# A start without unread matmuls between the first scores, and the first weights behind the first pair

## The chip, the cores and the metric

The kernel runs on one core of a Trainium2 chip. The metric is the device time of one launch in microseconds (us): the median over several executions. The engines of the core are named as in the profile: PE (TensorE, with PEld for its weight loads), DVE (VectorE), ACT (ScalarE), POOL (GpSimd) and SP (SyncE, which issues the DMAs here). Each runs its own list of instructions in order.

## What is computed

Attention with a forget gate for 8 batches of 8 heads, 576 positions, 64 dimensions a head, and then a two-layer feed-forward network over the 4608 tokens:

```python
scores = scale * np.matmul(q, k.transpose(0, 1, 3, 2))
log_f = np.log(np.clip(f, 0.0001, 1.0))
cum = np.cumsum(log_f, axis=-1)
decay = cum[:, :, :, None] - cum[:, :, None, :]
scores = np.where(causal, -1000000000.0, scores + decay)
scores = scores - np.max(scores, axis=-1, keepdims=True)
attn = np.exp(scores)
attn = attn / (np.sum(attn, axis=-1, keepdims=True) + 1e-09)
x = np.matmul(attn, v)            # heads side by side: 4608 x 512
h = x @ w_in                      # 512 x 2048
g = np.maximum(0.01 * h, h)
return g @ w_out                  # 2048 x 512
```

All is float32. The two weight matrices arrive as 64-bit integers.

## The kernel before

**The opening.** Batches are taken in the order 0, 3, 4, 5, 6, 7, 1, 2. Of the first three, only the first 256 positions are done at first, so that the feed-forward network gets its first tokens soon. This is the loop at line 732: twelve *pairs* of heads, four for each of the three batches. For each pair `early_load` (L287) fetches q, k and v. `early_scores` (L298) makes four score tiles, two heads by two row blocks of 128. Each is a matmul of q and k, the "q·k part" (`sce<-qk`), and a second one that adds the decay (`sce<-both`, "decay part"). DVE then adds the mask, reduces to the row's extreme and writes tile `ze` (L323), and ACT takes the exponential and the row sum (L327). When a pair's four tiles are done, DVE scales them by the inverse sums (L336; from the fifth pair on ACT does it, L338). `early_values` (L340), one pair later, transposes them on PE (`tre`), copies them (`pte`), multiplies by v (`ave`) and splits the result in a high and a low part (`xh`, `xl`), which the network's matmuls read.

**The weights** come in 16 pieces, w_in and w_out in turn. A piece is loaded raw (`wraw`, two DMAs of 512 KB at L167) into one of two buffers, used in turn: piece n + 2 can be loaded only when piece n has been read for the last time. `load_weight` (L169) turns it into two float tiles, high and low (`win_h`, `win_l`, `wout_h`, `wout_l`). ACT does L181 and L192. DVE does L185, L194, L195 for the first five pieces, and L187, L206, L207, L210, L211 for the others. For the first five pieces PE also sums three products into PSUM (`ws`, L201 to L203), and ACT and DVE copy one half each back (L204). The tile `wt` in the middle has one buffer, so the pieces pass through one after the other. The first two pieces are fetched ahead of the loop. `WQ` says how many pieces come behind each pair's scores: one each for the first eight pairs, then two. Piece 0 is worked on ahead of the loop, by `weights(1)` in L731.

**The network** is cut into quanta (`ffn`, L617): groups of 256 tokens; for each of eight pieces p of the hidden layer, matmuls into `h`, the activation `g` on ACT (L654), its split `gh`, `gl` (L657, L659), and matmuls into `o`. `fill` (L700) puts quanta behind each pair, from the fifth on, by the table `FQ`. After the opening comes the loop over the remaining heads (L755), with quanta between all steps.

**Unread matmuls.** `warm(n)` (L119) multiplies a tile of zeros into a PSUM tile that nobody reads. `WARM = (20, 2, 6)` asks for 20 of them at the very start, and for 2 behind each of the two row blocks of each of the first 6 pairs (L330).

**The order.** A scheduling layer places the instructions of each engine, in the order of the program as far as its own plan of readiness allows. Since the unread matmuls depend on nothing but a free PSUM tile, 20 of the 24 later ones were placed around pair 0's first scores, the last four at pair 5's.

Of the kernel before, what the change touches and what calls it, by code (L numbers as in the profile page):

```python
# [28 lines left out]
FQ = (0, 0, 0, 0, 4, 8, 8, 8, 8, 8, 8, 4, 2)  # L29
BUFS = dict(s1=2, m1=2, ost=2)  # L30
RAWS = ("ph", "pl")
WARM = (20, 2, 6)
SCALED = 4
SUMMED = 5
NEG = -1.0e30
# [5 lines left out]
def forgetting_attention_ffn(ctx, tc, qT, kT, v4, vr, f, w_in, w_out, out):  # L41
# [77 lines left out]
    def warm(n):  # L119

        ps = psum.tile([P, 512], F32, tag="h", name=f"warm_{len(warmed)}")
        warmed.append(n)
        for _ in range(n):
            matmul(ps, still[:, :P], still, start=True, stop=True)

    warm(WARM[0])
    eye = one.tile([P, P], F32, tag="part0", name="eye")
# [36 lines left out]
    def fetch_weight(n):  # L164
        raw = raws[n] = one.tile([P, 2, 4 * P, 2], I32, tag=RAWS[n % 2], name=f"wraw_{n}")
        for k, src in enumerate(wpieces[n][0]):
            nc.sync.dma_start(raw[:, k].rearrange("p w two -> p (w two)"), src)  # L167
# [47 lines left out]
    def weights(n):  # L215
        while len(loaded) < min(n, len(wpieces)):
            load_weight(len(loaded))
# [80 lines left out]
    def early_scores(b, g):  # L298
# [3 lines left out]
        for i in range(2):  # L302
# [14 lines left out]
            for o in range(2):  # L317
# [11 lines left out]
                )  # L329
            if b * HPB // 2 + g < WARM[2]:  # L330
                warm(WARM[1])
        nc.vector.tensor_scalar(sm, sm, 1.0e-9, None, op0=ALU.add)
# [395 lines left out]
    early_load(0, 0)  # L728
    for n in range(len(RAWS)):
        fetch_weight(n)  # L730
    weights(1)  # L731
    for x, (b, g) in enumerate(steps + [(NE, 0)]):
        if x + 1 < len(steps):
            early_load(*steps[x + 1])
# [91 lines left out]
```

## Time and profile before

| | |
|---|---|
| median of 3 executions | 1208.28 us (1208.0 to 1208.91) |
| the profiled execution | 1209.36 us |
| its span, first to last instruction | 1207.5 us |
| PE busy | 1194.9 us, 7828 matmul records |
| DVE busy | 613.2 us |
| ACT busy | 633.2 us |
| unread matmuls, all 44 | 13.2 us of PE's records |

A row of the timeline reads: start, duration, engine, line, operation, output <- input, shapes, count, and in brackets the idle time of the engine ahead of it with what ended it. Matmuls overlap: the duration of a merged row reaches past the start of the next row, so a stretch of PE is measured from one row's start to the next one's. A float32 matmul that isn't marked fp32r shows as two records.

### The profile page before, as it was taken

How to read it: one execution, taken by the hardware profiler on the slowest of the kernel's cores; microseconds unless marked ns; L12 is line 12 of the kernel's file. 1: busy time of each engine (PE TensorE's matmuls, PEld its weight loads, DVE VectorE, ACT ScalarE, POOL GpSimd, SP SyncE). 2: the span in 40 equal slices, each digit the busy share in tenths (PEclk: the TensorE clock that was granted, in tenths of full speed). 3: DMA queues.
4: the chain of work that ended last, by engine and by line, in shares of the span. 5: the costliest groups of instructions: out<-in, count | busy, mean ns of one | idle time of the engine just before them, and what ended most of it. 6: DMA issues, size and time to landing. Idle time of an engine off the chain costs nothing.

```text
span 1207.5 us, 22521 instructions
## 1 busy us (share of the span) xinstructions
PE 1194.9 (99%) x7828; PEld 1068.1 (88%) x7828; DVE 613.2 (51%) x1697; ACT 633.2 (52%) x1622; POOL 460.8 (38%) x473
## 2 busy tenths in 40 slices
PE   9999999999999999999999999999999999999998
PEld 6678888888899999999999999999999999998997
DVE  6888365566655555464544445444443434553221
ACT  5887465666755565555554545455444445552111
POOL 2000255555455445454435354444354543531000
PEclk9999999999999999999999999999999999999999
DMA  6565233334343233323332223232233223311000
GB/s 202 175 204 177 78 99 101 99 111 118 102 137 82 82 99 101 99 72 97 87 96 79 80 66 101 65 100 59 69 85 93 58 71 81 80 58 52 13 18 19
DMA packets 82130, 110.57 MB, mean 92 GB/s; under 512 B 20640, under 2 KB 51728, under 8 KB 82016
## 3 DMA queue, kind: packets, MB, share of 16 engines
q1 hardware_dynamic: 82016, 109.12, 31.2%
q8 instruction: 63, 1.03, 0.4%
q14 instruction: 51, 0.42, 0.1%
HBM read 65.32 MB, written 18.58 MB: 69 GB/s over the span
## 4 chain that ended last, share of the span: by engine, by line
PE 95%; DVE 2%; ACT 1%; DMA 1%; issue 1%; POOL 0%; SPq 0%; DVEq 0%; ACTq 0%; POOLq 0%
PE h L111 34%; PE o L111 33%; PE tr L115 8%; PE av L111 8%; PE sc L111 7%; PE sce L111 2%; PE ave L111 1%; PE ws L111 1%; PE warm L111 1%; PE tre L115 1%; DVE fixed_z L437 1%; DMA wraw<-in_w_in 0%; ACT g L654 0%; DVE pl L489 0%; DVE gh L657 0%
## 5 line engine op out<-in xcount | busy, mean ns | idle before, releaser
L659 POOL TENSOR_TENSOR gl<-g,gh 128x512 fp32r<-128x512 f32 x113 | 148.8, 1317 | 275.1 <-DVE gh L657 270.1
L111 PE MATMUL o<-wout_h,gh 128*128 128x512 f32 x576 | 231.3, 402 | 0.0
L111 PE MATMUL o<-wout_l,gh 128*128 128x512 f32 x576 | 227.4, 395 | 0.0
L111 PE MATMUL o<-wout_h,gl 128*128 128x512 f32 x576 | 227.1, 395 | 0.0
L443 ACT ACTIVATE fixed_z<-fixed_z,max 128x192 f32<-128x192 f32 (+3 forms) x272 | 161.0, 592 | 101.4 <-DVE max L437 99.1
L111 PE MATMUL h<-xh,win_h 128*128 128x256 f32 x1152 | 206.2, 286 | 0.0
L487 ACT CAST ph<-tr 128x192 fp32r<-128x192 f32 (+3 forms) x360 | 126.7, 373 | 148.5 <-PE tr L115 99.2
L111 PE MATMUL h<-xh,win_l 128*128 128x256 f32 x1152 | 200.3, 283 | 0.0
L437 DVE CUSTOM_DVE_ANT_0 fixed_z<-sc,tri 128x192 f32<-128x192 f32 (+3 forms) x272 | 122.4, 451 | 151.3 <-PE sc L111 148.4
L654 ACT ACTIVATE g<-h 128x512 f32<-128x512 f32 x144 | 85.8, 596 | 216.1 <-PE h L111 211.0
L657 DVE CAST gh<-g 128x512 fp32r<-128x512 f32 x144 | 72.4, 503 | 217.6 <-ACT g L654 215.9
L489 DVE TENSOR_TENSOR pl<-tr,ph 128x384 fp32r<-128x384 f32 (+3 forms) x296 | 137.3, 467 | 80.7 <-ACT ph L487 79.5
L111 PEld LDWEIGHTS h<-xh,win_h 128*128 128x128 f32 x1152 | 170.8, 190 | 5.8 <-issue 0.5
L111 PEld LDWEIGHTS h<-xh,win_l 128*128 128x128 f32 x1152 | 164.8, 190 | 0.5 <-issue 0.2
L111 PE MATMUL h<-xs,win_h 128*128 128x256 f32 x1024 | 164.4, 283 | 0.0
L115 PE MATMUL tr<-ident_r,fixed_z 128*128 128x128 f32 x888 | 145.3, 273 | 3.4 <-DVE ph L494 1.7
L111 PEld LDWEIGHTS h<-xs,win_h 128*128 128x128 f32 x1024 | 141.0, 191 | 0.0
L115 PEld LDWEIGHTS tr<-ident_r,fixed_z 128*128 128x128 f32 x888 | 107.6, 140 | 25.2 <-ACT rb L566 5.2
L111 PEld LDWEIGHTS o<-wout_h,gl 128*128 128x128 f32 x576 | 108.2, 188 | 24.4 <-DVE maxe L323 0.3
L111 PEld LDWEIGHTS o<-wout_l,gh 128*128 128x128 f32 x576 | 108.7, 189 | 16.0 <-issue 0.5
L111 PEld LDWEIGHTS o<-wout_h,gh 128*128 128x128 f32 x576 | 108.9, 189 | 14.8
L154 POOL TENSOR_TENSOR fixed_m2a<-raw,m 64x576 fp32r<-64x576 f32 x32 | 46.6, 1458 | 195.4 <-ACT m L399 173.8
(130 smaller groups left out, 1753.2 us busy)
## 6 DMA issues: line engine op xcount, KB each, us to landing
raw<-in_kT SPq DMA_DIRECT2D x64, 144.0 KB
m<-m SPq DMA_DIRECT2D x64, 144.0 KB
wraw<-in_w_in SPq DMA_DIRECT2D x16, 512.0 KB
wraw<-in_w_out SPq DMA_DIRECT2D x16, 512.0 KB
fixed_vm<-in_v SPq DMA_DIRECT2D x64, 128.0 KB
xs<-xd SPq DMA_DIRECT2D x16, 512.0 KB
out<-ost SPq DMA_DIRECT2D x28, 256.0 KB
raw<-in_qT SPq DMA_DIRECT2D x40, 144.0 KB
```

What stands on the lines that cost most here:

```text
L111: nc.tensor.matmul(*args, **kw)
L115: nc.tensor.transpose(*args)
L154: nc.gpsimd.tensor_tensor(out, a, b, op=ALU.subtract)
L437: nc.vector.tensor_tensor_reduce(out=z[:, a:b], in0=ps[:m, :b - a], in1=tri[:m, at:at + b - a], scale=-SCALE, scalar=3.0e38 if x == 0 else ...
L443: nc.scalar.activation(z, z, AF.Exp, bias=h["max"][:m, last:last + 1], scale=-1.0, accum_out=fixed["sum" + "ab"[s // 2 % 2]][:m, i, s % 2: ...
L487: nc.scalar.copy(strided(ph, run), source(ps, run))
L489: nc.vector.tensor_tensor(strided(pl, run), source(ps, run), strided(ph, run).bitcast(F32), op=ALU.subtract)
L654: nc.scalar.activation(g, ph, AF.Prelu, alpha=0.01)
L657: nc.vector.tensor_copy(gh, g)
L659: eng.tensor_tensor(gl, g, gh.bitcast(F32), op=ALU.subtract)
```

## The change

Two edits. The table `WARM` becomes (20, 0, 0): the 20 unread matmuls at the very start stay, the 24 behind the row blocks of the first six pairs are gone. And `weights(1)` ahead of the loop is gone, so that piece 0 is worked on where the loop asks for it, behind pair 0's scores. The load of pieces 0 and 1 stays ahead of the loop.

```diff
@@ -29,7 +29,7 @@
 FQ = (0, 0, 0, 0, 4, 8, 8, 8, 8, 8, 8, 4, 2)
 BUFS = dict(s1=2, m1=2, ost=2)
 RAWS = ("ph", "pl")
-WARM = (20, 2, 6)
+WARM = (20, 0, 0)
 SCALED = 4
 SUMMED = 5
 NEG = -1.0e30
@@ -728,7 +728,6 @@
     early_load(0, 0)
     for n in range(len(RAWS)):
         fetch_weight(n)
-    weights(1)
     for x, (b, g) in enumerate(steps + [(NE, 0)]):
         if x + 1 < len(steps):
             early_load(*steps[x + 1])
```

The scheduling layer places all else anew. On PE, the list around pair 0's first scores was this, from the last of nine rows of two unread matmuls that stood behind the two q·k parts (`sce` with `_0` and `_2` are the first row block's scores, `_1` and `_3` the second's):

```order
L111 MATMUL warm_511<-still 128x512 x2
L111 MATMUL sce_0_0_216<-both 128x128
L111 MATMUL sce_0_2_217<-both 128x128
L111 MATMUL warm_526<-still 128x512 x2
L111 MATMUL sce_0_1_231<-qk_0_182 128x256
L111 MATMUL sce_0_3_232<-qk_0_182 128x256
L111 MATMUL ws_0_199<-wt_193,ident_r 128x512
```

and it is now:

```order
L111 MATMUL sce_0_0_200<-qk_0_182 128x128
L111 MATMUL sce_0_2_201<-qk_0_182 128x128
L111 MATMUL sce_0_0_200<-both 128x128
L111 MATMUL sce_0_2_201<-both 128x128
L111 MATMUL sce_0_1_212<-qk_0_182 128x256
L111 MATMUL sce_0_3_213<-qk_0_182 128x256
L111 MATMUL sce_0_1_212<-both 128x256
L111 MATMUL sce_0_3_213<-both 128x256
L111 MATMUL sce_1_0_253<-qk_1_193 128x128
```

The four scores of pair 0 now stand together, pair 1's follow at once, and piece 0's sums (`ws`) stand behind pair 1's four scores. Further changes of the order, on DVE, are shown in the prediction at the places where it speaks of them. From the first head of the second loop on, the lists of PE are the same again.

## The prediction

> **What bounds the kernel now.** I read the page first, for the engine that carries the span.
>
> ```profile
> span 1207.5 us, 22521 instructions
> PE 1194.9 (99%) x7828; PEld 1068.1 (88%) x7828; DVE 613.2 (51%) x1697; ACT 633.2 (52%) x1622; POOL 460.8 (38%) x473
> PE 95%; DVE 2%; ACT 1%; DMA 1%; issue 1%; POOL 0%; SPq 0%; DVEq 0%; ACTq 0%; POOLq 0%
> ```
>
> PE is busy 99% of the span, and 95% of the chain that ended last runs on it. So an edit at the start is worth what it takes off the time at which PE gets through the same list of matmuls, and nothing else. Then I read the stretches of the opening.
>
> ```profile
> 13.30:45.60 32.30, 31.36 (x140) 17.87 (x139) 26.97 (x87) 24.67 (x63) 0.00 (x0) 1.00 0.53 172
> 45.60:57.20 11.60, 11.60 (x85) 9.76 (x84) 10.82 (x25) 8.67 (x19) 0.00 (x0) 1.00 0.50 182
> 57.20:98.00 40.80, 40.76 (x254) 31.25 (x252) 35.51 (x85) 32.50 (x79) 0.00 (x0) 1.00 0.62 202
> ```
>
> Columns: stretch, length, busy PE, PEld, DVE, ACT, POOL, granted clock, DMA share, GB/s. From 13.3 us PE is idle for only 0.94 us up to 45.6, and hardly at all after it. DVE is close behind: it idles 5.33 us in the first stretch, 0.78 in the second, 5.29 in the third. Both have to be ahead for the end to move. Last I read the opening instruction by instruction, PE first.
>
> ```profile
> 8.31 0.49 PE L111 MATMUL sce<-qk 64*128 64x128 f32 x4
> 8.73 4.38 PE L111 MATMUL warm<-still 128*128 128x512 f32 x18
> 12.95 0.34 PE L111 MATMUL sce<-both 128*128 128x128 f32 x2
> 13.12 0.68 PE L111 MATMUL warm<-still 128*128 128x512 f32 x2
> 13.73 0.85 PE L111 MATMUL sce<-qk 64*128 64x256 f32 x4
> 14.51 1.12 PE L111 MATMUL ws<-wt,ident_r 128*128 128x512 f32 x2
> 17.48 0.40 PE L111 MATMUL sce<-both 128*128 128x256 f32 x2
> 18.76 0.48 PE L111 MATMUL sce<-qk 64*128 64x128 f32 x2 [0.89 <-DVE maxe L323]
> ```
>
> Eighteen unread matmuls stand inside pair 0's first scores, between the q·k part (8.31) and the decay part (12.95). DVE shows what that costs:
>
> ```profile
> 13.32 0.29 DVE L323 CUSTOM_DVE_ANT_0 ze<-sce,tri 128x128 f32<-128x128 f32 x1 [4.68 <-PE sce L111]
> 13.75 0.69 DVE L185 TENSOR_SCALAR wt<-wt 128x1024 int32<-128x1024 int32 x1
> 15.20 1.23 DVE L195 SCALAR_TENSOR_TENSOR win_l<-wraw 128x1024 fp32r<-128x1024 uint32 x1
> 17.68 0.69 DVE L204 CAST win_l<-ws 128x512 fp32r<-128x512 f32 x1 [1.25 <-PE ws L111]
> 18.28 0.41 DVE L323 CUSTOM_DVE_ANT_0 ze<-sce,tri 128x256 f32<-128x256 f32 x1
> 18.97 0.69 DVE L185 TENSOR_SCALAR wt<-wt 128x1024 int32<-128x1024 int32 x1
> 19.57 0.28 DVE L323 CUSTOM_DVE_ANT_0 ze<-sce,tri 128x128 f32<-128x128 f32 x1
> 44.43 1.22 DVE L195 SCALAR_TENSOR_TENSOR win_l<-wraw 128x1024 fp32r<-128x1024 uint32 x1
> ```
>
> It waits 4.68 us for that score, then does piece 0 of the weights (13.75 to 18.28) before pair 0's second half at 18.28.
>
> **The change, part by part.** *The eighteen in front.* Without them the decay part can start at 8.73 instead of 12.95, so DVE's first score comes 4.2 us earlier, near 9.1. By the distances of the rows (DVE 13.32, next q·k 13.73, then 0.78 and the decay part) pair 0's second half is through PE near 10.5 and through DVE near 11.5. That is where the gain stops, since next on PE and on DVE stands pair 1, whose q and k are not there yet:
>
> ```profile
> 6.48 0.44 SPq L292 DMA_DIRECT2D qk<-in_kT  x1
> 9.96 1.13 ACT L181 ACTIVATE wt<-wraw 128x1024 f32<-128x1024 f32 x1 [1.77 <-DMA wraw<-in_w_in]
> 12.00:13.00 1.00, 1.00 (x6) 0.81 (x6) 0.00 (x0) 0.00 (x0) 0.00 (x0) 1.00 0.78 251
> 13.00:14.00 1.00, 1.00 (x7) 0.64 (x7) 0.68 (x5) 0.29 (x1) 0.00 (x0) 1.00 0.10 32
> ```
>
> They were issued at 6.48 behind two whole weight pieces; the first of these reaches ACT at 9.96, and the queue runs dry only just after 13. SP issues in the same order in the new kernel, so I take 13.3 for pair 1 (12.3 to 13.8 possible). Of the 4.2 us, PE keeps what it has done by 13.3: pair 0's second scores, 14.51 − 13.73 = 0.78 and some 0.24 of decay part, and the two unread matmuls at 13.12, 0.61. That is 1.6 us. DVE has its four scores done, 0.43 (13.32 to 13.75) + 0.69 (18.28 to 18.97) = 1.1 us.
>
> *Piece 0 behind pair 0.* On DVE the rows move so; `ze` is a score, `wt`, `wraw`, `win_l` are weights. Before:
>
> ```order
> L323 ISA ze_0_2_225,maxe_0_214<-sce_0_2_217,tri 128x128
> L323 ISA maxe_0_214 128x1
> L185 TENSOR_SCALAR wt_193<-wt_193 128x1024
> L194 TENSOR_SCALAR wraw_187<-wt_193 128x1024
> L195 SCALAR_TENSOR_TENSOR win_l_108<-wraw_187 128x1024
> L204 CAST win_l_108<-ws_1_204 128x512
> L323 ISA ze_0_1_237,maxe_0_214<-sce_0_1_231,tri 128x256
> ```
>
> And now, from pair 1's third score on:
>
> ```order
> L323 ISA ze_1_1_271,maxe_1_251<-sce_1_1_265,tri 128x256
> L323 ISA maxe_1_251 128x1
> L336 TENSOR_SCALAR ze_0_0_206<-ze_0_0_206,sume_0_199 128x128
> L336 TENSOR_SCALAR ze_0_1_218<-ze_0_1_218,sume_0_199 128x256
> L336 TENSOR_SCALAR ze_0_2_209<-ze_0_2_209,sume_0_199 128x128
> L336 TENSOR_SCALAR ze_0_3_221<-ze_0_3_221,sume_0_199 128x256
> L185 TENSOR_SCALAR wt_230<-wt_230 128x1024
> L323 ISA ze_1_3_274,maxe_1_251<-sce_1_3_266,tri 128x256
> ```
>
> Piece 0 now waits behind seven scores and pair 0's scaling. Its wait for PE (1.25 at 17.68) goes, but DVE has nothing between 11.5 and pair 1, and after that no weights to fill its gaps. All that piece 0 issues moves, L181, L192 and L204 on ACT, L185 to L204 on DVE, and its matmuls on PE; its own load does not, since it is fetched ahead of the loop. Its last reading of the raw tile, 15.20 before, moves by my count to about 18.8, so SP's load of piece 2 into that buffer is 3.6 us later. On SP pair 3's q and k now stand ahead of that load, and pair 3's v between its two halves, so the second half also waits for pair 0's v to be read.
>
> I make the sum as a ledger to the end of piece 4's L195 (44.43 + 1.22, so 45.6), because up to there DVE's set of instructions is the same in both orders. Before: 26.97 busy + 5.33 idle. After: 26.97 − 1.1 = 25.9 of work from 13.3 on, plus waits. Those I count from the new order with the durations above: 0.8 until pair 1's first score (18.76 on PE to 19.57 on DVE); 0.9 for its next scores, which PE now does one by one; 1.6 where piece 1's L204 stands ahead of pair 2's last score and its matmuls behind that pair's on PE; and 1.9 in smaller ones, at pieces 2 and 3 and pair 4. Together 5.2, an estimate. 13.3 + 25.9 + 5.2 = 44.4: a lead of 1.2 to 1.3. PE's ledger gives the upper end: 1.6, and at most all its idle time of 0.94, so 2.6. If my waits are 2 us short, as a late piece 2 would make them, the lead is −0.6. I take 1.3, because the next 50 us need DVE (10.82 of 11.60 busy).
>
> *The four at 54 and 56.*
>
> ```profile
> 54.45 0.63 PE L111 MATMUL warm<-still 128*128 128x512 f32 x2
> 55.01 0.70 PE L111 MATMUL sce<-qk 64*128 64x256 f32 x4
> 55.98 0.63 PE L111 MATMUL warm<-still 128*128 128x512 f32 x2
> 56.46 0.82 PE L115 MATMUL tre<-ident_r,ze 128*128 128x128 f32 x6
> 56.47 0.42 DVE L323 CUSTOM_DVE_ANT_0 ze<-sce,tri 128x256 f32<-128x256 f32 x1
> ```
>
> These stand in PE's unbroken stretch and take 0.56 + 0.48 = 1.04. But DVE takes the score between them only at 56.47, when it has finished other work, so part of it returns as a wait. Between 0 and 1.04; I take 0.5.
>
> *A wait further on.* PE's one wait near 110 us comes from the weights:
>
> ```profile
> 110.36 1.13 ACT L181 ACTIVATE wt<-wraw 128x1024 f32<-128x1024 f32 x1 [3.03 <-DMA wraw<-in_w_in]
> 112.14 0.69 DVE L206 TENSOR_SCALAR wraw<-wraw 128x1024 int32<-128x1024 int32 x1
> 112.74 0.28 DVE L323 CUSTOM_DVE_ANT_0 ze<-sce,tri 128x128 f32<-128x128 f32 x1
> 113.09 0.91 PE L111 MATMUL sce<-qk 64*128 64x256 f32 x4 [0.80 <-DVE maxe L323]
> ```
>
> ACT waits 3.03 us for piece 14, DVE's L206 of it stands ahead of pair 10's first score, and PE waits 0.80. On DVE before, `win_l_114` being piece 12, the next 13, `wraw_1516` 14:
>
> ```order
> L211 SCALAR_TENSOR_TENSOR win_l_114<-wraw_1347 128x1024
> L187 TENSOR_SCALAR wt_1361<-wt_1361 128x1024
> L206 TENSOR_SCALAR wraw_1358<-wraw_1358 128x1024
> L207 SCALAR_TENSOR_TENSOR wraw_1358<-wraw_1358 128x1024
> L657 CAST gh_2_1240<-g_2_1238 128x512
> L210 TENSOR_SCALAR wraw_1358<-wt_1361 128x1024
> L211 SCALAR_TENSOR_TENSOR wout_l_130<-wraw_1358 128x1024
> L187 TENSOR_SCALAR wt_1519<-wt_1519 128x1024
> L206 TENSOR_SCALAR wraw_1516<-wraw_1516 128x1024
> L323 ISA ze_2_0_1312,maxe_2_1304<-sce_2_0_1306,tri 128x128
> ```
>
> And now:
>
> ```order
> L211 SCALAR_TENSOR_TENSOR win_l_114<-wraw_1311 128x1024
> L187 TENSOR_SCALAR wt_1325<-wt_1325 128x1024
> L206 TENSOR_SCALAR wraw_1322<-wraw_1322 128x1024
> L323 ISA ze_2_0_1276,maxe_2_1268<-sce_2_0_1270,tri 128x128
> ```
>
> The score moves ahead of piece 14, to behind the start of piece 13, whose data come a piece earlier. The 0.80 should go (0 to 1.0 with the row of distance after it). Late next is pair 11, whose first score now stands behind the start of piece 15, the last; if that comes as late as piece 14 did, the 0.80 is back. I take 0.8, since PE has pair 10 and its feed-forward work to do in between.
>
> *Sum.* 1.3 + 0.5 + 0.8 = 2.6, ends −0.6 and 4.6. The profiled execution took 1209.36 with a span of 1207.5; the shift takes the span to 1204.9, the execution to 1206.8. The median, 1208.28, goes to 1205.7. From pair 11 on PE's order is as before, and PE has no slack that could swallow a lead.
>
> *The clock.* The first twenty unread matmuls, which stay, show PE starting slowly, though the granted clock reads 1.00 throughout:
>
> ```profile
> 1.45:5.88 4.43, 4.43 (x10) 3.47 (x11) 1.00 0.63 180
> 5.88:8.31 2.43, 2.43 (x11) 1.72 (x9) 1.00 1.02 374
> ```
>
> Ten take 4.43 us, the next ten 2.43. Now PE pauses from about 10.6 to 13.3, 2.7 us. The Trainium skill, page TensorE: Matmul & The Clock Gate, section "Why this matters for your kernels", wants no idle gap above about 3 us, else the array falls back to half rate; by that rule the pause is just short enough and the sum stays 2.6 us, while with a slightly later landing it would be the second rival's. No trace here shows a gap of this size.
>
> **The rivals.** *Eaten up (0.21).* DVE's counted waits are 1 to 2 us too low, PE waits for scores, and the four at 54 come back as waits: about 1208, no change. For it: DVE is 93% busy from 45.6 to 57.2. Against it: it then idles 5.29 us to 98, where it can catch up.
>
> *Slow clock (0.13).* PE falls back in the pause. At 4.43 against 2.43 for the same work, a slow stretch loses 0.45 of its length. If PE recovers after one stretch like the first 4.43 us, that is 2.0 us, and the time is 1207.7 (0.06). If its work stays too broken, it could last to about 30 us: 16 × 0.45 = 7.2, and 1205.7 + 7.2 = 1212.9 (0.07). It decides for slower from (2.6 + 2.4) / 0.45 = 11 us on. Against it: the pause is 2.7 us, and PE works on both sides of it.
>
> *Late weights (0.04).* Each load waits for its buffer and SP is in order, so a late piece 0 could push all 16: 5 us of PE waiting at the first `h` matmuls, 1210.7. Against it: by my count piece 3 is level again.
>
> *The whole shift (0.07).* Nothing takes back the 4.2 us of the first score: 4.2 + 1.0 + 0.8 = 6.0, so 1202.3. Against it: pair 1's load, above.
>
> **How the numbers follow.** 0.2% is 2.4 us, about what a measurement of this kernel can tell from no change. The forecast holds 0.55, its own range 1203.7 to 1208.0; 0.46 of it lies below 1205.9, 0.09 within 0.2%. Faster: 0.46 + 0.07 = 0.53. Same: 0.09 + 0.21 + 0.06 = 0.36. Slower: 0.07 + 0.04 = 0.11. The range goes from 1202.3, the whole shift, to 1209.6, a little above no change, and leaves out the two slower cases.
>
> **What would show it.** Right: DVE's first score near 9.1, pair 1's first on DVE near 14, piece 4's L195 ending near 44.4, no PE wait near 110, matmuls of 512 columns still about 0.23 us apart after 13 us. Wrong: a wait above 2 us on DVE between 20 and 45; 0.43 between such matmuls; ACT waiting for piece 2 or 3; PE no earlier at pair 11 than before.

## The result, and the profile after

| | before | after |
|---|---|---|
| median, us | 1208.28 (1207.43 to 1208.91, five executions) | 1216.99 (1216.48 to 1218.05, five) |
| ratio of after to before | 1 | 1.0075, 95% interval 1.0060 to 1.0090 |
| profiled execution, us | 1209.36 | 1216.93 |
| its span, us | 1207.5 | 1215.1 |
| its mean granted clock | 1.000 | 0.996 |

The change makes the kernel slower by 8.7 us; the forecast was 2.6 us faster. All medians and ratios here are of fast executions; one slow execution of E9 below (1525.6 us at a clock of 0.702) is left out. The opening went as far as pair 0 about as the prediction says. PE's instructions in the timeline after (start, length, instruction, count, in brackets the idle time ahead and who ended it):

```profile
9.10 0.49 PE L111 MATMUL sce<-qk 64*128 64x128 f32 x4
9.52 0.44 PE L111 MATMUL sce<-both 128*128 128x128 f32 x2
...
11.19 0.51 PE L111 MATMUL sce<-both 128*128 128x256 f32 x2
14.38 0.69 PE L111 MATMUL sce<-qk 64*128 64x128 f32 x2 [2.69 <-DMA qk<-in_kT]
14.99 0.47 PE L111 MATMUL sce<-both 128*128 128x128 f32 x1
15.40 0.79 PE L111 MATMUL sce<-qk 64*128 64x128 f32 x2
16.12 0.47 PE L111 MATMUL sce<-both 128*128 128x128 f32 x1
```

The eighteen unread matmuls are gone from between 9.10 and 9.52, pair 0 is through near 11.7, and PE waits 2.69 us for pair 1's kT, as forecast. But two q·k records of pair 1 now take 0.69 and 0.79 us, where two of them took 0.48 in before (18.76 in the prediction's rows). The same stretch by windows of 3.41 us, the unit in which stretches of half clock come in these traces (columns as in the prediction; the granted clock is the third number from the end):

```profile
7.63:11.05 3.42, 3.02 (x17) 2.03 (x15) 1.34 (x7) 1.21 (x5) 0.00 (x0) 1.00 0.99 364
11.05:14.46 3.41, 0.72 (x4) 0.41 (x4) 0.78 (x4) 2.31 (x7) 0.00 (x0) 1.00 0.77 263
14.46:17.87 3.41, 3.41 (x9) 2.08 (x9) 0.86 (x6) 0.99 (x4) 0.00 (x0) 0.50 0.03 9
17.87:21.29 3.42, 3.42 (x10) 2.10 (x11) 3.00 (x11) 0.60 (x2) 0.00 (x0) 0.50 0.22 62
21.29:24.70 3.41, 3.41 (x10) 1.86 (x8) 2.38 (x8) 2.29 (x5) 0.00 (x0) 0.50 0.36 113
24.70:28.11 3.41, 3.41 (x17) 1.60 (x15) 1.17 (x4) 2.33 (x5) 0.00 (x0) 1.00 0.14 55
```

PE is busy for 0.72 us of the window that holds the pause, and right behind it the clock is at one half for three such windows, 10.24 us. Nothing in the engine columns says so: PE reads 3.41 of 3.41, with 10 matmuls where the next window at full clock has 17. The prediction let DVE wait 5.2 us from 13.3 on to the end of piece 4's L195. It waits much longer, mostly for PE. Its chief waits from 13.3 to 52.5, where piece 4 now ends (us, times, longest):

```profile
DVE ze L323 <- PE sce L111: 6.5, 5, 3.1
DVE wout_l L204 <- PE ws L111: 3.3, 2, 2.3
DVE win_l L204 <- PE ws L111: 2.5, 2, 2.2
DVE sume L332 <- ACT ze L327: 1.0, 1, 1.0
```

Together that is 13.3 us. Piece 4 ends 6.8 us later than before (52.41 against 45.65), pair 5's first score on PE 5.5 us later (55.63 against 50.12), pair 10's 8.4 us later (118.98 against 110.63), and from the first head of the second loop to the end the distance stays between 7.5 and 8.5.

What the lag consists of can be counted at pair 11's first score, up to which both lists hold the same records but for the 24 unread ones. PE gets there 7.6 us later (135.15 against 127.52). Its idle time up to there is 4.3 us instead of 1.8: 2.5 us, mostly the pause. The 10.24 us at half clock lose half their length: 5.1 us. That is all of it. So the unread matmuls, 5.9 us by the prediction's rows, saved nothing: as much was added elsewhere. From the start of one record to the next, idle time and half the half clock taken off, the twenty unread matmuls that stay take 0.8 us more in this execution, the value matmuls 2.5, the q·k parts of the scores 1.5, the network's matmuls 1.1.

Two more things are seen only when the traces are laid beside each other. The first is how long the value matmuls take. An early pair has four (eight records, 64 columns of the array each), two per head. In most pairs of before the two heads stood together; in after most are pulled apart. Before:

```profile
33.37 1.25 PE L111 MATMUL ave<-pte,ve 128*64 128x256 f32 x8
34.55 0.33 PE L115 MATMUL tre<-ident_r,ze 128*128 128x128 f32 x1
```

After, one head at a time:

```profile
33.77 0.86 PE L111 MATMUL ave<-pte,ve 128*64 128x256 f32 x4
34.57 0.49 PE L111 MATMUL sce<-qk 64*128 64x128 f32 x4
...
37.99 0.86 PE L111 MATMUL ave<-pte,ve 128*64 128x256 f32 x4
38.79 0.48 PE L111 MATMUL sce<-qk 64*128 64x256 f32 x1
```

From the first record to the next instruction it is 1.18 us for both heads together, and 0.80 for each head by itself, 1.6 for the two: side by side the second head overlaps the first. In the order of before the four stand unbroken in 8 of 12 pairs, in that of after in 2. Up to pair 11 the 80 records take, before and after (busy time; counted from start to start, 12.7 and 15.2):

```profile
0.00:127.50 127.50, 13.63 (x80) 1.00 0.56 185
```

```profile
0.00:135.10 135.10, 16.59 (x80) 0.96 0.53 174
```

The same holds for the q·k parts of the two heads of a row block, which use 64 rows of the array each. In after, one head alone, and further on both together:

```profile
27.68 0.49 PE L111 MATMUL sce<-qk 64*128 64x128 f32 x2
28.10 0.33 PE L111 MATMUL sce<-both 128*128 128x128 f32 x1
...
34.57 0.49 PE L111 MATMUL sce<-qk 64*128 64x128 f32 x4
34.99 0.44 PE L111 MATMUL sce<-both 128*128 128x128 f32 x2
```

Two records take 0.42 us, and so do four. Up to pair 11 the two heads stand together in 18 of 22 row blocks in before, in 15 in after.

The second is the last piece. The SP queue after:

```profile
124.95 0.33 SPq L167 DMA_DIRECT2D wraw<-in_w_out  x1
...
127.25 0.59 SPq L360 DMA_DIRECT2D xd<-xe  x1
127.89 0.43 SPq L167 DMA_DIRECT2D wraw<-in_w_out  x1
```

and what hangs on it, from the timeline of all engines:

```profile
133.92 1.13 ACT L181 ACTIVATE wt<-wraw 128x1024 f32<-128x1024 f32 x1 [1.61 <-DMA m<-m]
135.09 0.73 DVE L187 TENSOR_SCALAR wt<-wt 128x1024 int32<-128x1024 int32 x1 [2.80 <-ACT wt L181]
135.15 0.49 PE L111 MATMUL sce<-qk 64*128 64x128 f32 x4
...
137.63 0.29 DVE L323 CUSTOM_DVE_ANT_0 ze<-sce,tri 128x128 f32<-128x128 f32 x1
```

Half of piece 15 is issued behind the transfer of a result (`xd`), 2.9 us after the other half. ACT's row names `m`, a transfer that shares a semaphore with the first half; the second half's own semaphore is complete at 133.76, just ahead of ACT's start. DVE then waits 2.80 us for ACT, and pair 11's first score stands behind that: DVE takes it 2.5 us after PE began it, where before it was 0.8 (127.52 on PE, 128.30 on DVE). PE's lag grows by 0.9 us behind that, from 7.6 to 8.5. The last piece ends at 140.0 instead of 123.1.

### The profile page after: what moved, and what is told of

Read it like the earlier page. It is cut to its first block, busy times and chain, and to the rows that moved or that the text cites. A ratio compares the mean times of both kernels' runs of the same rounds, so it can differ in the third digit from the quotient of the medians.

```text
span 1215.1 us, 22475 instructions
## 1 busy us (share of the span) xinstructions
PE 1199.8 (99%) x7804; PEld 1068.8 (88%) x7804; DVE 617.6 (51%) x1697; ACT 632.4 (52%) x1622; POOL 461.3 (38%) x473
## 4 chain that ended last, share of the span: by engine, by line
PE 93%; DVE 2%; ACT 2%; DMA 1%; SPq 1%; issue 1%; POOL 0%; ACTq 0%; DVEq 0%; POOLq 0%
PE h L111 33%; PE o L111 32%; PE tr L115 8%; PE av L111 8%; PE sc L111 7%; PE sce L111 2%; PE ave L111 1%; PE ws L111 1%; DMA qk<-in_kT 1%; PE tre L115 1%; DVE fixed_z L437 0%; ACT g L654 0%; ACT wt L181 0%; DMA wraw<-in_w_out 0%; DVE pl L489 0%
## 5 line engine op out<-in xcount | busy, mean ns | idle before, releaser
L657 DVE CAST gh<-g 128x512 fp32r<-128x512 f32 x144 | 75.7, 525 | 213.3 <-ACT g L654 211.8
```

Source lines behind the costliest of these rows:

```text
L657: nc.vector.tensor_copy(gh, g)
```

## The experiments

Theory C: the time is lost to the half clock. Theory W: it is lost because the new order of the pieces makes the weights late, whatever the clock. Theory T, which came with the traces: the new order pulls apart matmuls that ran side by side, which below is called torn. Each kernel was timed in five rounds beside before, which had medians of 1208.09 to 1208.95 there. Each edit leaves the rest of the source alone, but the scheduling layer may place other instructions anew. Where single executions are told, "clock" is the mean granted clock of that execution, to three digits.

### The clock in the opening

**E1: more unread matmuls at the start**, so that PE gets to pair 0 later and pair 1's load is there.

```diff
-WARM = (20, 0, 0)
+WARM = (32, 0, 0)
```

> The changed kernel with 32 instead of 20 unread matmuls at the very start; the order on every engine is that of the changed kernel, only the run at the start is 12 matmuls, some 2.8 us, longer. Theory C (clock): the changed kernel's loss comes from PE's pause of 2.69 us ahead of pair 1, after which the granted clock reads 0.5 for 10.24 us. Here PE reaches pair 0 near 11.9 us and its pause is under 1 us, so the clock stays at 1.0, and the time is 1205 to 1209. Theory W (weights behind scores): the new order itself puts the weight pieces later, and PE waits behind them between 70 and 120 us whatever the clock does: 1212 to 1217 with the clock at 1.0.

Measured: 1215.73 (1215.02 to 1216.97), ratio 1.0060 (1.0048 to 1.0072). In the opening PE has no gap over 0.4 us any more, and still:

```profile
12.07:15.48 3.41, 3.01 (x14) 1.92 (x14) 1.45 (x11) 2.54 (x9) 0.00 (x0) 1.00 0.50 157
15.48:18.89 3.41, 3.41 (x10) 1.81 (x8) 2.73 (x12) 1.72 (x7) 0.00 (x0) 0.50 0.07 18
```

Half clock for 6.83 us, from 15.48 on. The pause is not what it takes: the clock fell behind a window in which PE counts as busy for 3.01 us with small matmuls. Neither theory had its condition, a clock at 1.0.

**E2: pair 1's loads ahead of the weights.**

```diff
     early_load(0, 0)
+    early_load(*steps[1])
...
-        if x + 1 < len(steps):
+        if 0 < x < len(steps) - 1:
```

> The changed kernel with pair 1's q, k and v issued ahead of the two weight pieces; the order on PE, DVE and ACT is that of the changed kernel. Theory C: pair 1's data are there near 7 us, PE has no pause ahead of pair 1, the clock stays at 1.0, and the time is 1203 to 1207. The first weights land some 1 us later, which nothing notices. Theory W: the clock stays at 1.0 too, but the pieces are late by the order: 1211 to 1216.

Measured: 1214.08 (1212.89 to 1214.78), ratio 1.0043 (1.0031 to 1.0055). Pair 1's first score on PE is at 11.67 instead of 14.38, no gap of the opening is over 0.4, and the clock is at one half from 13.52 to 20.34. Same answer. Beside before, E2 is 3.9 us faster than after was; in the traces PE's idle time up to pair 5 is 2.3 us less (0.8 instead of 3.1), and the half clock costs 1.7 us less (half of 3.41).

**E9: four unread matmuls that can't be moved ahead**, since they read what DVE has just written. Nothing else in the source differs from after.

```diff
-            if b * HPB // 2 + g < WARM[2]:
-                warm(WARM[1])
+            if b == 0 and g < 2:
+                ps = psum.tile([P, 512], F32, tag="h", name=f"fill_{g}_{i}")
+                matmul(
+                    ps[:2, :512], mx[:, i::2], still.bitcast(F32)[:, :512], start=True, stop=True
+                )
```

> The kernel after and nothing else but the four fp32 matmuls of 512 columns whose result is not read, behind the row blocks of pairs 0 and 1 (3.4 us of PE's time); pair 1's loads stay behind the weights. Theory C, in the form that a window of 3.41 us with too little streamed lets the clock fall: PE's hole before pair 1 now holds one of the four, and if the clock holds the time goes from 1217 to what the run with pair 1 first has shown at full clock, 1208.5, plus at most 1: 1209. If it still falls for one or two windows: 1211 to 1213. Theory that PE's hole itself is the loss (the 2.7 us wait for pair 1's q and k, which the four don't shorten): 1215 to 1217.

Measured: 1213.5 (1209.56 to 1217.13, six executions), ratio 1.0039 (1.0023 to 1.0055). Two executions at clock 1.000 took 1209.56 and 1209.73; four at 0.996 and 0.997 took 1213.32 to 1217.13. The trace is of one of the latter:

```profile
8.90:12.32 3.42, 2.72 (x9) 0.97 (x8) 0.89 (x7) 0.88 (x4) 0.00 (x0) 1.00 1.04 389
12.32:15.73 3.41, 2.79 (x10) 1.34 (x10) 2.37 (x13) 2.50 (x7) 0.00 (x0) 1.00 0.27 82
15.73:19.14 3.41, 3.41 (x15) 1.92 (x15) 2.49 (x7) 2.56 (x7) 0.00 (x0) 1.00 0.00 0
111.31:114.72 3.41, 1.56 (x14) 1.24 (x12) 1.84 (x3) 2.31 (x3) 0.00 (x0) 1.00 0.41 157
114.72:118.13 3.41, 3.08 (x10) 1.46 (x12) 3.38 (x8) 2.75 (x7) 0.00 (x0) 0.50 0.00 0
```

The clock holds through the opening. Although the four take 3.8 us of PE (0.95 each), pair 5's first score is at 49.20, 6.4 us earlier than in after, and pair 6's too (66.57 against 72.96). Of this, 5.1 us is the half clock that is not there and 1.6 is idle time (1.5 instead of 3.1). The time of the four is made up for elsewhere: the first twenty unread matmuls took 1.0 us less in this execution, and the order is not that of after (pair 2's first score stands behind two pieces' sums, at 26.14 instead of 19.84). So E9 changes more than the clock, but C holds for the opening, without the pause as its condition. What is left is a later fall: ACT waits 3.87 us for a weight piece until 111.65, PE waits 2.17 us, until 115.05, for a copy that ACT makes behind it, and the clock falls at 114.72.

**E7: E9 with E2's loads.**

> The kernel after with pair 1's loads ahead of the weights, as in the second experiment, and one unread 512-column fp32 matmul behind each row block of pairs 0 and 1 that reads what DVE has just written, so that it can't be moved ahead: four of 0.85 us, 3.4 us of PE's time, which is about what 6.8 us of half clock cost there. Theory C: the clock stays at full rate, and then nothing is left that is dearer than before: at most 1208.7, and by the fit of the third experiment's runs (1206.8 at full clock) plus 3.4 less PE's idle time down to 1207. Theories W and T: the clock holds, and the new order still costs what the fourth experiment's one run at full clock showed, 1212.5 against 1208.7, 3.8 us: 1211 to 1213.

Measured: 1209.35 (1208.18 to 1212.35), ratio 1.0010 (1.0001 to 1.0019); the profiled execution, at 1208.18, has no half clock at all. That is above what C allowed, 1208.7 at most, but nearer to it than to W's and T's 1211 to 1213. It doesn't set T aside: the order is that of E9, in which fewer products are torn, and the value matmuls up to pair 11 take 14.48 us instead of 16.59. With the clock held and this order, the kernel is about level with before, with 3.8 us of unread work still in it.

**E11: four more behind pairs 9 and 10**, on E10 below.

```diff
-            if b == 0 and g < 2:
+            if (b * HPB // 2 + g) in (0, 1, 9, 10):
```

> The kernel of the run before with four more such unread matmuls, behind the row blocks of pairs 9 and 10, where the clock fell near 114 us in the tied kernel and in the third experiment's. They cost up to 3.4 us of PE's time there, less what PE waits anyway (1 to 2 us). If the late fall costs more than that in most executions: faster than the run before by 1 to 3; if it is rare once the early part is quick: slower by 1 to 2, and a narrower spread of the times.

Measured: 1213.23 (1210.06 to 1217.37), ratio 1.0039 (1.0026 to 1.0053), slower than either theory gave. Two executions at clock 1.000 took 1210.06 and 1210.15, 2 us above E10's at that clock, which may be the price of the added matmuls. The other six ran at 0.996 to 0.998, with a fall at 96.0 in the trace, so the added ones don't prevent a late fall either.

### One part of the change alone

**E3: only the unread matmuls gone**; piece 0 stays ahead of the loop.

```diff
-WARM = (20, 2, 6)
+WARM = (20, 0, 0)
```

> The kernel before without the 24 unread matmuls; piece 0 stays ahead of the loop. PE pauses after pair 0's first scores until piece 0's wt is made, near 12.5 us, about 2.3 us. Theory C: it is the pause that decides; at 2.3 us it may be just too short for the clock to fall, then 1203 to 1206; if the clock reads 0.5 again, 1211 to 1217. Theory W: the order of the weights is that of before, so no piece is late: 1203 to 1207, whatever the clock reads.

Measured: 1211.34 (1207.56 to 1215.03, twelve executions), ratio 1.0022 (1.0010 to 1.0034). The spread is the clock:

| clock | 0.999 | 0.998 | 0.997 | 0.996 | 0.995 | 0.994 |
|---|---|---|---|---|---|---|
| us | 1207.56, 1207.72 | 1209.33, 1209.53, 1209.67 | 1211.19, 1211.49 | 1213.02, 1213.54 | 1212.46 | 1214.46, 1215.03 |

A line through the twelve gives 1206.8 at full clock and 1.38 us for each 0.001 (correlation 0.96). 0.001 of some 1210 us is 1.21 us of PE's time, so most of the price is plain half speed. By the line, the kernel without the 24 would take 1206.8 at full clock, 1.5 to 1.9 us less than before (no execution of it had full clock). W gave 1203 to 1207 whatever the clock, so the spread speaks for C. The last piece ends 11.3 us late here too (134.34 against 123.08), in a kernel that the line puts ahead of before.

**E4: only piece 0 behind pair 0**, all unread matmuls kept.

```diff
-    weights(1)
     for x, (b, g) in enumerate(steps + [(NE, 0)]):
```

> The kernel before with piece 0 behind pair 0's scores and all 24 unread matmuls kept; 18 of them stand between the two parts of pair 0's first scores, as before, so PE works until near 13 us. Theory C: no pause above 1.5 us, clock at 1.0, 1206 to 1210. Theory W: the pieces are as late as in the changed kernel: 1212 to 1217.

Measured: 1213.71 (1212.49 to 1216.05), ratio 1.0045 (1.0033 to 1.0057). One execution at clock 1.000 took 1212.49, so by this one execution this half of the change costs 3 to 4 us without any half clock: W or T, not C. Its pieces come late, the last by 12.6 us. In its trace PE is 3.8 us late at pair 11: 1.7 is half clock, 1.0 idle time, and 1.1 the matmuls, among them 1.8 more for q·k parts, of which 15 of 22 row blocks stand together, as in after. The value matmuls take no longer than in before (13.65 us). And the clock falls here too, with all unread matmuls kept, behind a window in which PE counts as busy nearly throughout:

```profile
14.67:18.08 3.41, 3.39 (x13) 2.10 (x14) 2.17 (x13) 3.35 (x11) 0.00 (x0) 1.00 0.13 38
18.08:21.50 3.42, 3.42 (x11) 2.33 (x12) 3.24 (x9) 2.00 (x6) 0.00 (x0) 0.50 0.27 77
```

**E8: E3 with E2's loads.**

> The third experiment's kernel (the 24 unread matmuls gone, the first piece still ahead of the loop) with pair 1's q, k and v loaded ahead of the weights. On PE, DVE and ACT the order is that of the third experiment. Theory C: what the time does hangs on the stretch of half clock alone; at 1.4 us for each 0.001 of mean clock and 1206.8 at full clock, the time is read off the clock, within 0.7; if the earlier pair 1 fills PE's hole at 11 to 15 us, the clock holds and the median falls from 1211.3 to about 1207. Theory W: the pieces come later by the 2 us that pair 1's three loads take on the queue, and the time is no better than 1211 whatever the clock.

Measured: 1213.62 (1210.43 to 1214.42), ratio 1.0032 (1.0020 to 1.0045), clock 0.995 to 0.998. The clock did not hold, so the hope of 1207 fell. The rule half held: 1206.8 + 5 × 1.38 = 1213.7 for 0.995, where 1213.62 and 1214.42 were measured, but the other three are 0.8 to 1.4 us above it (1213.76 at 0.996, 1211.76 at 0.997, 1210.43 at 0.998), more than the 0.7 that was allowed. So the time follows the clock, with about 0.8 us on top in this kernel.

### The torn matmuls

**E5: after, with the four value matmuls of a pair tied together.** The head whose operand comes last goes first, the other is pinned behind it.

```diff
-        for o, pt in enumerate(pts):
+        for o in (1, 0):
             rows_ = slice(o * D, (o + 1) * D)
-            matmul(out[rows_, :T], e["v"][:, o, 0], pt[:, :T], start=True, stop=False)
-            matmul(out[rows_, P:T], e["v"][:, o, 1], pt[:, T:], start=False, stop=True)
+            a = matmul(out[rows_, :T], e["v"][:, o, 0], pts[o][:, :T], start=True, stop=False)
+            if o == 0:
+                tc.keep_in_program_order(a)
+            a = matmul(out[rows_, P:T], e["v"][:, o, 1], pts[o][:, T:], start=False, stop=True)
+            tc.keep_in_program_order(a)
```

> The kernel after, with one edit: the four value matmuls of an early pair (`ave`) are tied together on PE, so that the two heads' products, which fill different halves of the array's columns, stand next to each other. In the order of before 8 of the 12 pairs have them together, in the order of after only 2. Theory T (torn groups: the new order pulls apart matmuls that ran side by side, and PE has no slack to pay for it): a group together takes about 1.2 us and a torn one 1.6, so some 7 groups that come together again give 2 to 3 us: 1214 to 1215, with the clock as after has it. Theory C (all of the loss is the half clock) and theory W (all of it is late pieces of weights): no change, 1217 within 1, unless the stretch of half clock changes too, which the trace would show.

Measured: 1210.89 (1208.72 to 1213.24, eleven executions), ratio 1.0018 (1.0010 to 1.0027): 6.1 us less than after, at a clock of 0.994 to 0.997 (after: 0.994 to 0.996). T, and twice as much as T gave. Both heads now take 0.81 us, in the nine of twelve pairs where they stand unbroken:

```profile
36.19 0.88 PE L111 MATMUL ave<-pte,ve 128*64 128x256 f32 x8
37.00 0.48 PE L111 MATMUL sce<-qk 64*128 64x256 f32 x1
```

and the 80 records up to pair 11

```profile
0.00:128.90 128.90, 10.18 (x80) 0.95 0.56 182
```

10.18 instead of 16.59 us, 6.4 less (5.8 from start to start), about as much as the whole gain. So the torn products are a price that the half clock, as low here as in after, doesn't explain.

**E6: before with the same tie.**

> The kernel before, with the same edit and nothing else: its 4 torn groups of value matmuls come together, and in the new order 2 torn pairs of score products are left instead of 5. Theory T: 4 x 0.35 us and 3 x 0.4 us, about 2.6 us faster: 1206. Theories C and W: the clock of before never falls and its pieces of weights stay where they are, so 1208.7 within 0.8.

Measured: 1207.96 (1206.42 to 1212.23), ratio 0.9998 (0.9989 to 1.0007). The records take 9.87 instead of 13.63 us, and in the trace PE leads by 4.6 us at pair 8, but is 1.1 us late at pair 10, the clock having been at one half from 94.8 to 101.7. Five executions at clock 1.000 took 1206.42 to 1207.62, the others, at 0.996 to 0.999, up to 1212.23. T's gain is there up to pair 9 and then mostly lost; the last piece ends 9.6 us later than in before.

**E10: all three edits, E2's loads, E9's four matmuls, the tie.**

> The kernel after with three edits together: pair 1's loads ahead of the weights, the four unread matmuls that hold the clock, and the value matmuls of a pair tied together. Theories C and T together: the run with the first two had 1208.4 at full clock and 13.4 us of value matmuls on PE up to pair 11, the tied ones take 9.3; 4.1 us less make 1204.4, and 1204.5 is also what the tied kernel's runs give when fitted to full clock; with a short late fall of the clock in some executions, 1204 to 1207. Theory W (what is left is set by when the weights come): 1208 to 1209, as without the tie.

Measured: 1208.04 (1206.27 to 1209.27), ratio 0.9998 (0.9989 to 1.0006), outside what C and T gave and within W's 1208 to 1209. PE is 4.3 us ahead of before at pair 11 and level at the first head of the second loop. DVE in between:

```profile
124.16 0.70 DVE L187 TENSOR_SCALAR wt<-wt 128x1024 int32<-128x1024 int32 x1 [3.17 <-ACT wt L181]
...
126.72 0.28 DVE L323 CUSTOM_DVE_ANT_0 ze<-sce,tri 128x128 f32<-128x128 f32 x1
```

and the clock there:

```profile
123.91:127.33 3.42, 1.74 (x15) 1.53 (x15) 3.13 (x8) 2.30 (x5) 1.78 (x5) 1.00 0.24 67
127.33:130.74 3.41, 3.41 (x15) 1.84 (x14) 2.67 (x5) 0.60 (x4) 0.00 (x0) 0.50 0.02 5
```

It is the last piece, as in after: pair 11's score is on PE at 123.26 and on DVE 3.5 us later. PE is idle for 1.68 us behind that, and the clock falls right after that window.

### The late weights

**E12, E13, E14, E15: the loads of pieces 2 to 15 issued by POOL**, in after, in before, in E10 and in E6.

```diff
-            nc.sync.dma_start(raw[:, k].rearrange("p w two -> p (w two)"), src)
+            (nc.gpsimd if n > 1 else nc.sync).dma_start(
+                raw[:, k].rearrange("p w two -> p (w two)"), src
+            )
```

> The kernel after with the loads of pieces 2 to 15 issued by POOL, which has nothing else to do between 10 and 117 us, instead of SP, where the second half of the last piece stands behind a transfer that waits for pair 9's result. Theory W: the pieces come as their buffers come free; the last one ends near 130 us instead of 140, and of the 3.5 us that the new order costs at full clock most goes: 1213 to 1215 with the early fall of the clock as it was. If the weights' lateness costs nothing: 1216 to 1218.

> The control: the kernel before with the loads of pieces 2 to 15 issued by POOL and nothing else. If its pieces are late too (ACT waited 3.0 us for piece 14 and PE 0.8 us behind it): 1206 to 1208. If a load on that queue starts later or the change of queue disturbs the order: 1209 to 1212. If neither: 1208.3 within 0.8.

> The kernel with pair 1's loads first, the four unread matmuls that hold the clock and the tied value matmuls, now with the weight loads on POOL. Theory W: it led by 4.3 us at pair 11 and lost that behind the last two pieces, so most of the lead stays: 1204 to 1205.5. If the lead is lost to something else between pair 11 and the long stage: 1207 to 1208.5, as it was.

> The kernel before with tied value matmuls and the weight loads on POOL. It led by 4 to 4.9 us from pair 7 to pair 8 without POOL and was level at pair 10. Theory W: 1203.5 to 1205.5. Otherwise: 1207 to 1208, as the tied kernel's runs at full clock.

Measured: E12 1219.38 (1218.83 to 1220.70), ratio 1.0090 (1.0077 to 1.0103). E13, the control, 1212.37 (1209.82 to 1213.97), 1.0030 (1.0019 to 1.0041), three of six executions at clock 1.000 and 1211.67 to 1212.52. E14 1210.44 (1205.97 to 1212.85), 1.0010 (1.0000 to 1.0020). E15 1209.54 (1207.19 to 1211.74), 1.0009 (1.0000 to 1.0017). All four medians lie above every range that was forecast for them. The control alone loses 3 to 4 us, so the move has a price of its own, and the four are no evidence on W. In the trace of E12 the pairs' own loads now come late, which may be part of the price. PE's largest wait from 8 to 150 us:

```profile
PE sce L111 <- DMA qk<-in_kT: 7.4, 3, 3.1
```

E14 has two executions at clock 1.000, 1205.97 and 1206.02, where E10 had 1207.49 and 1208.36; the other ten, at 0.995 to 0.998, took 1209.00 to 1212.85.

**E16, E17, E18: one transfer alone, the second half of piece 15, issued by POOL**, in E10, in after and in E6 (the condition above is `n == 15 and k`).

> The kernel with pair 1's loads first, the four unread matmuls that hold the clock and the tied value matmuls, with one transfer moved: the second half of piece 15 is issued by POOL, all others by SP as before. Theory W in its narrow form: ACT's L181 of piece 15 comes right behind piece 14 instead of 3 to 5 us later, DVE does pair 11's first score at once, PE has no hole of 3 us near 125 and the clock stays up there; 3 to 4 us come off the runs at full clock and more off those that fell: 1204 to 1205. If the lead is lost elsewhere: 1207 to 1208.5.

> The kernel after with the second half of piece 15 issued by POOL and nothing else. Narrow W: pair 11's first score is no longer 2.5 us behind PE's, 1.5 to 2.5 us come off: 1214.5 to 1215.5, with the early fall of the clock as it was. Otherwise 1216 to 1218.

> The kernel before with the tied value matmuls and the second half of piece 15 issued by POOL. Without the latter it gave 1207.96, 1207.3 at full clock, and led by 3.8 to 4.9 us from pair 7 to pair 9. Narrow W: most of 3 us come off: 1204 to 1205.5. Otherwise 1207 to 1208; PE's wait at pair 10, which this edit doesn't touch, may keep part of it.

Measured: E16 1206.40 (1204.36 to 1210.80), ratio 0.9991 (0.9981 to 1.0001). E17 1219.51 (1217.67 to 1221.01), 1.0095 (1.0081 to 1.0108). E18 1207.98 (1205.75 to 1210.11), 0.9999 (0.9990 to 1.0008). In E16 DVE waits less for the piece:

```profile
124.53 0.69 DVE L189 TENSOR_SCALAR wt<-wt 128x1024 int32<-128x1024 int32 x1 [0.62 <-ACT wt L183]
...
127.73 0.28 DVE L325 CUSTOM_DVE_ANT_0 ze<-sce,tri 128x128 f32<-128x128 f32 x1
```

0.62 instead of 3.17 us, and pair 11's score is 1.6 us behind PE (126.16) instead of 3.5. PE itself is 2.9 us later there than in E10's trace, with half clock from 96.4 to 99.8. Its four executions at clock 1.000 took 1204.36 to 1206.16, against 1207.49 and 1208.36 in E10. So the narrow W is likely there, for about 2 us by these few executions; the median lies between the two forecasts. In after (E17) the same edit gains nothing, and narrow W's condition did not come: the half piece, issued by POOL at 122.68, lands 7.9 us later, at 130.63 (issued by SP in after it took 5.9), and pair 11's first score is on DVE 3.25 us behind PE (135.85 against 132.60) instead of 2.5. The profiled execution leads after by 2.6 us at pair 11, but it does so from pair 5 on, having had 6.83 us of half clock in the opening; at the next stage it is level, the clock having fallen once more at 137.3. E18 is what it was. E16 has the lowest median of all, but its interval reaches 1.0001, and 1.0 is in it; a version that beats before is not shown.

## Why the prediction was wrong, point by point

- **"The clock": failed, and it is the largest step.** The prediction had the pause at 2.7 us (2.69 measured) and kept the array at full rate with it, against its rival at 0.13. The clock fell. The condition that it went by does not decide: by the Trainium skill, page TensorE: Matmul & The Clock Gate, section "Why this matters for your kernels", an idle gap above about 3 us brings the fall, and here it came behind 2.69 us, and in E1 and E2 in an opening without any gap above 0.4. The measurements decide: a pause is not needed. The busy time of the window ahead doesn't decide either: the clock fell behind 0.72 us (after), 3.01 (E1, E2) and 3.39 (E4) of 3.41, and held behind 2.72 and 2.79 in E9 and 2.52 in before. What the traces show is that the clock held through the opening in every one with before's source there, tied or not, and in every one with E9's four; in E4, with all unread matmuls kept but piece 0 moved, it fell. In the profiled execution the half clock takes 5.1 of PE's 7.6 us of lag at pair 11, and the pause nearly all of the other 2.5. So without the half clock PE would, by this count, still be late instead of early: the second failed step is "piece 0 behind pair 0", below. The rival that had it, at 0.13, reckoned with 0.45 of a stretch's length, 4.6 us for these 10.24, and 7.2 at most; its time of 1212.9 falls short in part because it left the forecast's gain of 2.6 in place.
- **"The eighteen in front" and "the four at 54 and 56": right in sum, in part by luck.** Forecast 1.3 + 0.5; E3, with this edit alone, gives 1.5 to 1.9 together by its line. But of the four at 54 next to nothing stays: in E3 PE is 0.17 us early at pair 5 and 0.26 at pair 6, so the eighteen make up nearly all of it, 1.9 at pair 5 with the 1.7 us added that half clock cost up to there. In after, with both edits, nothing of either is left at pair 11. DVE's first score came at 10.00 instead of 9.1, since PE's start was 0.8 us later in that execution; it is 0.9 us behind PE's first score, where 0.8 was forecast.
- **"Piece 0 behind pair 0": failed.** The ledger counted the same PE work in a new order at the same price, and set a loss at 0.6 at most. E4 shows 3 to 4 us in one execution at full clock. In after the value matmuls take 2.5 us more and the q·k parts 1.5, since neighbours that overlapped are torn. For the q·k parts this edit alone does it (E4, 1.8); for the value matmuls neither edit alone does (13.65 us in E4, 13.47 in E3), only both together. Piece 0's L195 was to come at 18.8 and came at 21.41; DVE's waits from 13.3 to piece 4 were 13.3 us in the four groups shown instead of 5.2, mostly for PE, which paused or ran at half clock.
- **"A wait further on": half right, and no gain.** At pair 10 PE's 0.80 us is gone as such: after shows no idle time of PE between 110 and 120. But PE waits 0.62 us at 105.60 for a copy of ACT, which before doesn't, and 0.49 at 74.55. And the prediction's own caution, pair 11 behind the last piece, came true: 2.5 us from PE's score to DVE's. E10 also answers "PE has no slack that could swallow a lead": its lead of 4.3 us at pair 11 is gone at the first head of the second loop.
- **"Late weights", at 0.04: the pieces came late, but not at this price.** The count that had piece 3 level again is wrong: piece 3 ends 7.1 us late and the last 16.9. But after has no wait of PE for weights at the first `h` matmuls: its waits from 8 to 128 us are 2.7 us for pair 1's kT, 0.9 for DVE and 0.6 for ACT. PE itself is 5.5 us late at pair 5, so much of the lateness follows the clock. What lateness itself costs is seen at the last piece alone: the 0.9 us behind pair 11's score.
- **A slip in the numbers.** The lower end of the sum, −0.6, gives 1208.9, where the forecast's own range ends at 1208.0. Nothing hangs on it.

Over all executions: after's five had a mean clock of 0.9946, which at E3's 1.38 us per 0.001 is 7.4 us. With −1.5 for the unread matmuls and +2.5 for the torn value matmuls that makes +8.4, with 8.7 measured. The terms were measured in different kernels and leave out the pause and the q·k parts, so the agreement is partly luck; after's own executions don't show that slope (1216.93 at 0.996, 1216.48 at 0.995, 1216.99 to 1218.05 at 0.994). The count in the trace is the firmer one. Open: the exact condition of the fall; why the two edits together tear the value matmuls; and why E13 pays 3 to 4 us.

## What to carry to other kernels

Unread matmuls may hold the granted clock long after the start. Before removing them, don't ask only for the longest gap: here the clock also fell without one. Give a stretch of half clock its price, about half of its length, and after the edit read the clock column in windows of some 3.4 us. When a scheduler is free to reorder, compare not only who waits but also which neighbours run side by side: the same matmuls took 10.2, 13.6 or 16.6 us here. A lead on the bounding engine can be lost to one transfer that a later step waits for, as E10's was.

## What the runs showed of the hardware that was not expected

- The granted clock fell to one half without a pause of PE: E1 from 15.48 on, behind a window with PE busy for 3.01 of 3.41 us, E4 from 18.08 on, behind one with 3.39. The half clock lasted whole windows, 3.41, 6.83, 10.24 or, in E12, 13.65 us.
- Two fp32 products of 64 columns each, on different halves of the array's columns, take 0.81 us in E5's order and 0.90 to 1.18 in that of before, both unbroken, and 1.6 apart, for the same eight records. Two q·k products of 64 rows each take 0.42 us together and 0.42 each alone (128 columns).
- The profile's busy column does not show a halved clock (PE 3.41 of 3.41 with 10 matmuls, then with 17), only the clock column does.
- Moving the weight loads from SP's queue to POOL's cost before 3 to 4 us (E13), though half of its executions ran at clock 1.000. The half piece that POOL issued took 7.9 us to land in E17 and 5.0 in E16.
